# The epsilon of the denominators on VectorE, and a fixed order table in place of a list scheduler, in a fused attention and token-mixing kernel

## The chip, the cores and the metric

The kernel runs on one core of a Trainium2 chip. The metric is the device time of one execution in microseconds (us). The profiled span is about 1.8 us shorter than the device time. Runs come in two states, by the clock that TensorE was granted and by the time: a run over 1.5% above the fastest of the same kernel is called slow, and only fast runs are compared.

Engine names in the profile: PE is TensorE's matmuls, PEld its weight loads, DVE is VectorE, ACT is ScalarE, POOL is GpSimd, SP is SyncE; a q after the name is the engine's issue of DMA transfers. L322 is a line of the source of that kernel, so the same instruction has another number in another kernel.

## The reference, cut to what matters

```python
# q, k, v: (8, 8, 576, 64) float32
def phi(x, c, s):                       # c, s: cos and sin of pi/2 * position / 576
    r = np.maximum(x, 0.0)
    return np.concatenate([r * c, r * s], axis=-1)
kv  = np.einsum('bhsf,bhsd->bhfd', k_p, v)
z   = np.sum(k_p, axis=2)
num = np.einsum('bhsf,bhfd->bhsd', q_p, kv)
den = np.einsum('bhsf,bhf->bhs', q_p, z)[..., None] + 1e-06      # <- the eps of the change
x   = (num / den)  # heads put side by side: (8, 576, 512)
W_tok = 1/8 * (x @ w_q) @ (x @ w_k).T   # written as an einsum
out = relu(W_tok @ x) @ w_out           # (8, 576, 512) float32
```

## The kernel before

Heads are taken in 16 pairs, H = 0 to 15, two of the eight heads of a batch at a time; two pairs at a time feed one of the eight token mixers b, and two mixers feed nine output blocks of 128 rows. The text uses the kernel's own short names:

- **load** of q, v, k (576 KB each, issued by SP); **rq, rv, rk**: relu or cast to bfloat16, on POOL or ACT; **mv**: value times cos and sin, DVE;
- **qT**: transposes of q on PE, **qe**: their eviction with cos and sin, DVE; **kv**: key-value product, **kve** its eviction; **num**: numerators and denominators on PE, **norm**: the division, DVE; **xT, xe**: transposes of x and their evictions;
- **wqk, we, wk, kx, mx, mxe**: the token mixer; **wo.p.n**: output block n of the p-th two mixers, **oe** its eviction to an output buffer, **st** its store; **warm**: dummy matmuls that only keep PE busy.

The eps came from four small matmuls at the end of each num:

```python
    # set up once
    ones_t = consts.tile([P, P], BF16);  nc.gpsimd.memset(ones_t, 1.0)
    eps_t = consts.tile([P, SC], BF16);  nc.gpsimd.memset(eps_t, 0.0)
    # ... two entries a half: EPS_HI and 1.0e-6 - EPS_HI
    def num_mm(H, m):
        # ... 40 matmuls of 64x65 over r, u, w, t, all with stop=False
        for r in range(2):
            for t in range(2):
                nc.tensor.matmul(nb[2 * t + r][:, :, D], ones_t[half_rows(t), :],
                                 eps_t[half_rows(t), :], start=False, stop=True)
    def norm(H, m):
        # ...
        nc.vector.reciprocal(rec, nv[:, :, :, D:D + 1])
        nc.vector.tensor_tensor(xv[:, h], nv[:, :, :, 0:D],
                                rec.to_broadcast([P, 4, SC, D]), op=ALU.mult)
```

The order of the work came from a list scheduler with tuned weights. Every engine, and the queue of loads and stores of SP, executes its part of that order strictly one after another:

```python
    def emit(n, eng, m):           # eng, m: engine and PSUM bank that the scheduler chose
        # ...
        elif kind == "oe":
            wout_evac(b, j, m, engs[eng])
            if b == B // 2 - 1 and j > 4:       # the last four blocks: a store right away,
                lo = (j - 5) % 2                # one half by SP, one by ACT
                store(b, (j + 1) // 2, (nc.sync, A), lo, lo + 1)
        elif kind == "st":
            if b < B // 2 - 1 or j < 3:
                store(b, j, (nc.sync, nc.sync))
        elif kind == "warm":
            warm_up(b, m)
    for n, eng, m in plan_order(NB):
        emit(n, eng, m)
```

## Time and profile before

| quantity | kernel before |
|---|---|
| median of its three first runs | 125.94 us (125.21 to 127.69) |
| the profiled run | 127.62 us, a **slow** one; span 125.8 us, mean clock 0.983 |
| start of kv.4, kv.5, num.15 | 34.80, 42.49, 105.28 us |
| last matmul ends; end of the span | 119.92; 125.84 us |

The start of a PE block in the span, as in the third row, is the ruler: the blocks are the same in both kernels, and where one of them comes later or earlier tells in which stretch the time went.

The profile that the prediction worked from is of a slow run. It has a spell of half clock from 32.8 to 36.2 us, and it is the only profile of this kernel, so whether its fast runs have one is not known. Its times fall roughly into two groups, in all calls: 125.2 to 126.8 and 127.1 to 128.1 us, with one of 130.2.

### The profile page before, as it was taken

What the parts mean: (1) busy time and instruction counts of PE and PEld (TensorE: products, weight loads), DVE (VectorE), ACT (ScalarE), POOL (GpSimd) and SP (SyncE); (2) the same over time, 40 slices, a digit from 0 to 9 for tenths busy, and PEclk for the clock granted to TensorE, in tenths of its full rate; (3) what the DMA queues carried; (4) which work ended last, traced back from release to release, by engine and by line L of the source; (5) the groups of instructions that cost most, each with busy time, mean ns of one, the idle gap of its engine ahead of it and who ended that gap; (6) DMA issues with size and microseconds to landing.
All of it is one profiled execution on the core that took longest, in us unless ns stands there. A gap on an engine that the chain in (4) does not pass through costs nothing.

```text
span 125.8 us, 4659 instructions
## 1 busy us (share of the span) xinstructions
PE 108.5 (86%) x1995; PEld 66.0 (52%) x1995; DVE 82.2 (65%) x90; ACT 83.7 (66%) x141; POOL 70.5 (56%) x113
## 2 busy tenths in 40 slices
PE   5958688688599989999999999999999988998910
PEld 1334454573166756657666666566656664543400
DVE  1064996988928988976878596869597973424000
ACT  5968365565258488786869686967696768756530
POOL 7730557429979998949898898578491000000000
PEclk9999999999779999999999999999999999999998
DMA  3999999999999999999999999999963601567784
GB/s 89 353 395 410 409 363 408 402 410 404 411 408 404 289 300 356 398 411 403 410 397 409 403 404 397 391 401 368 331 223 70 186 2 42 147 150 188 175 247 144
DMA packets 20788, 39.35 MB, mean 313 GB/s; under 512 B 2592, under 2 KB 4128, under 8 KB 20768
## 3 DMA queue, kind: packets, MB, share of 16 engines
q1 hardware_dynamic: 20176, 38.21, 85.2%
q10 hardware_dynamic: 592, 0.85, 2.1%
q8 instruction: 15, 0.25, 0.8%
q14 instruction: 5, 0.04, 0.1%
HBM read 29.62 MB, written 9.44 MB: 310 GB/s over the span
## 4 chain that ended last, share of the span: by engine, by line
PE 60%; DMA 12%; DVE 9%; ACT 9%; issue 2%; ACTq 1%; SPq 1%; POOL 1%; DVEq 0%; POOLq 0%
PE ps L559 25%; PE ps L429 11%; DMA raw<-in_q_dram 7%; PE ps L447 7%; PE ps L489 6%; DMA raw<-in_v_dram 4%; ACT kv_sb L367 4%; PE ps L519 4%; DVE x_sb L462 4%; DVE vp L393 3%; ACT o_sb L367 2%; PE ps L474 2%; PE ps L415 2%; PE ps L535 1%; DVE qpt_buf L421 1%
## 5 line engine op out<-in xcount | busy, mean ns | idle before, releaser
L559 PE MATMUL ps<-wo_sb,mix_sb 128*128 128x512 bf16 x144 | 36.4, 386 | 2.8 <-DVE mix_sb L549 1.4
L380 POOL TENSOR_SCALAR rq_buf<-raw 128x640 bf16<-128x640 f32 (+1 forms) x30 | 20.7, 706 | 14.4 <-DMA raw<-in_q_dram 14.2
L367 ACT COPY o_sb<-ps 128x512 f32<-128x512 f32 x36 | 21.0, 591 | 10.9 <-PE ps L559 9.2
L421 DVE TENSOR_TENSOR qpt_buf<-ps,cst 128x2304 bf16<-128x2304 bf16 x16 | 21.6, 1353 | 10.0 <-PE ps L415 9.5
L393 DVE TENSOR_TENSOR vp<-v_buf,cossin 128x2376 bf16<-128x2376 bf16 (+2 forms) x17 | 23.9, 1409 | 6.0 <-ACT v_buf L403 6.0
L380 POOL TENSOR_SCALAR rk<-raw 128x640 bf16<-128x640 f32 (+1 forms) x26 | 24.6, 964 | 3.2 <-DMA raw<-in_k_dram 1.9
L405 POOL TENSOR_SCALAR v_buf<-raw 128x640 bf16<-128x640 f32 (+1 forms) x28 | 21.4, 782 | 5.6 <-DMA raw<-in_v_dram 2.4
L462 DVE TENSOR_TENSOR x_sb<-ps,rec 128x1280 bf16<-128x1280 f32 x16 | 23.9, 1491 | 0.6
L429 PE MATMUL ps<-vp,rk 64*128 64x260 bf16 x288 | 19.9, 280 | 2.3 <-DVE vp L393 2.3
L559 PEld LDWEIGHTS <-mix_sb 128*128 128x128 bf16 x144 | 12.9, 98 | 17.2 <-issue 3.3
L547 ACT ACTIVATE mix_sb<-ps 128x576 bf16<-128x576 f32 x28 | 18.1, 660 | 2.6 <-PE ps L535 2.6
L367 ACT CAST kv_sb<-ps 128x520 bf16<-128x520 f32 x16 | 9.5, 592 | 13.9 <-PE ps L429 13.6
L429 PEld LDWEIGHTS <-rk 64*128 64x128 bf16 x288 | 13.5, 96 | 9.9 <-issue 2.5
L447 PEld LDWEIGHTS <-qpt_buf 64*128 64x128 bf16 x640 | 11.1, 94 | 4.5 <-issue 4.0
L367 ACT COPY xT_buf<-ps 128x640 bf16<-128x640 bf16 (+1 forms) x21 | 13.1, 655 | 0.4 <-PE ps L474 0.4
L447 PE MATMUL ps<-kv_sb,qpt_buf 64*128 64x65 bf16 x640 | 13.0, 190 | 0.0
L290 PE MATMUL ps<-warm 128*128 128x512 bf16 x35 | 10.6, 448 | 1.5 <-DVE warm L286 1.5
L415 PE MATMUL ps<-ident,rq_buf 64*128 64x64 bf16 x288 | 7.9, 191 | 2.4 <-POOL rq_buf L380 1.7
L489 PE MATMUL ps<-xT_buf,wqk_sb 128*128 128x288 bf16 x64 | 9.4, 286 | 0.0
L369 DVE COPY xT_buf<-ps 128x512 bf16<-128x512 bf16 (+1 forms) x11 | 4.8, 440 | 6.6 <-PE ps L474 5.1
L535 PE MATMUL ps<-wT_buf,kx 64*128 64x288 bf16 x32 | 8.3, 284 | 0.7 <-ACT mix_sb L547 0.4
L535 PE MATMUL ps<-wq,kx 64*128 64x288 bf16 x32 | 8.3, 284 | 0.4 <-ACT wq L367 0.4
(48 smaller groups left out, 94.8 us busy)
## 6 DMA issues: line engine op xcount, KB each, us to landing
raw<-in_q_dram SPq DMA_DIRECT2D x15, 576.0 KB, 8.2
raw<-in_v_dram SPq DMA_DIRECT2D x15, 576.0 KB, 7.3
raw<-in_k_dram SPq DMA_DIRECT2D x15, 576.0 KB, 8.0
out_dram<-o_sb SPq DMA_DIRECT2D x28, 256.0 KB, 5.4
out_dram<-o_sb SPq DMA_DIRECT2D x12, 128.0 KB, 3.6
wo_f<-in_moe_w_out_dram SPq DMA_DIRECT2D x1, 1024.0 KB, 8.4
out_dram<-o_sb ACTq DMA_DIRECT2D x4, 128.0 KB, 2.9
raw<-in_q_dram SPq DMA_DIRECT2D x1, 320.0 KB, 3.9
```

What stands on the lines that cost most here:

```text
L367: nc.scalar.copy(dst, src)
L380: eng.tensor_scalar(dst, src, FMAX, 0.0, op0=ALU.min, op1=ALU.max)
L393: nc.vector.tensor_mul(vp[H][:, 2 * lo:2 * hi], v_bufs[H % 3][:, lo:hi].rearrange("p c i d -> p (c i) d").unsqueeze(2) .to_broadcast([P, 2 ...
L405: eng.tensor_scalar(dst, src, 1.0, 1.0, op0=ALU.mult, op1=ALU.mult)
L421: nc.vector.tensor_mul(qpt_bufs[H % 2][:, :, :, D:SLOTS * D], bank_h(m, 2)[:, :, 0:HC].unsqueeze(2).to_broadcast([P, 2, 2, HC]), cst.unsqu ...
L429: nc.tensor.matmul(bank(m + r)[:, 0, 0:2 * KW], rks[H][half_rows(r), c, :, :], vp[H][half_rows(r), 2 * c:2 * c + 2, :, 0:D + 1], start=(c ...
L447: nc.tensor.matmul(nb[2 * t + r][:, u, :], qpt_bufs[H % 2][rows, r, w, u * P:(u + 1) * P], kvs[H][rows, r, k0:k0 + D + 1], start=(u == 0 a ...
L462: nc.vector.tensor_tensor(xv[:, h], nv[:, :, :, 0:D], rec.to_broadcast([P, 4, SC, D]), op=ALU.mult)
L489: nc.tensor.matmul(bank(m + nh)[:, 0, 0:hs], wqk_sb[:, dmc, :, :], xT_bufs[b % 2][:, dmc, nh * hs:(nh + 1) * hs], start=(dmc == 0), stop=( ...
L535: nc.tensor.matmul(bank(m + r)[:, 0, 0:hs], kxs[b][half_rows(r), i * P:(i + 1) * P], rhs, start=True, stop=True)
L547: nc.scalar.activation(dst, src, AF.Relu, scale=scale_moe)
L559: nc.tensor.matmul(bank(m)[:, 0, :], mixs[bp][:, dmc, rt * P:(rt + 1) * P], wo_sb[:, dmc, :], start=(dmc == 0), stop=(dmc == NDM - 1))
```

## The change

Its intent is to take the eps off PE, the fullest engine, and to replace the scheduler's order by one found offline, by annealing on a replay of the engines.

```diff
-def plan_order(NB, par=None):
-    ... (the list scheduler, some 170 lines)
+NRAW, NOUT = 7, 12
+ORDER = """
+load.q.1=S rq.1=A qT.0=P6 qe.0=V6 warm.3=P0 kv.0=P4 kve.0=A4 load.v.1=S load.k.1=S load.q.2=S
+... (473 items: what=engine and PSUM bank; S is SP's queue)
+... load.q.11=S mxe.2.1=A0 ... oe.0.8=V7 st.0.4=S rk.9=A xT.7=P2 xe.7.1=A3 rq.9=G
+load.v.11=S ...
+wo.3.6=P4 wo.3.7=P5 oe.3.2=A1 oe.3.3=V0 st.3.1=S oe.3.4=V6 st.3.2=S wo.3.8=P6 oe.3.5=V7
+oe.3.6=V4 st.3.3=S oe.3.7=V5 oe.3.8=A6 st.3.4=S
+"""
@@ num_mm
-                            kvs[H][rows, r, k0:k0 + D + 1], start=(u == 0 and w == 0), stop=False)
-        for r in range(2):
-            for t in range(2):
-                nc.tensor.matmul(nb[2 * t + r][:, :, D], ones_t[half_rows(t), :],
-                                 eps_t[half_rows(t), :], start=False, stop=True)
+                            kvs[H][rows, r, k0:k0 + D + 1], start=(u == 0 and w == 0),
+                            stop=(u == SC - 1 and w == 1))
@@ norm
-        nc.vector.reciprocal(rec, nv[:, :, :, D:D + 1])
+        nc.vector.tensor_scalar(rec, nv[:, :, :, D:D + 1], 1.0e-6, 1.0,
+                                op0=ALU.add, op1=ALU.mult)
+        nc.vector.reciprocal(rec, rec)
@@ (also gone: ones_t, eps_t and their six memsets)
-    for n, eng, m in plan_order(NB):
-        emit(n, eng, m)
+    for item in ORDER.split():
+        ... emit(n, on[where[0]], bank)
```

So two things change at once: the **eps part** (PE to DVE) and the **order**.

## The prediction

> **What bounds the kernel now.** I read the page first (engines and slices), then the stretches of the span, then the chain that ended last, then the order of PE's work in time with the start-to-start times of its blocks.
>
> The slices of the page for the kernel before: busy tenths of PE, the granted clock in tenths, and DMA, in slices of 3.145 us.
>
> ```profile
> PE   5958688688599989999999999999999988998910
> PEclk9999999999779999999999999999999999999998
> DMA  3999999999999999999999999999963601567784
> ```
>
> The same by stretches (us, busy us with instruction counts, clock, DMA share, GB/s), cut where the character changes:
>
> ```profile
> core 0: us, PE busy (x) PEld busy (x) DVE busy (x) ACT busy (x) POOL busy (x), PEclk, DMA share, GB/s
> 0.00:34.80 34.80, 26.06 (x460) 14.77 (x461) 23.57 (x26) 20.92 (x28) 20.38 (x51) 0.97 0.99 369
> 34.80:40.24 5.44, 5.43 (x113) 3.70 (x113) 2.81 (x2) 3.99 (x7) 4.71 (x7) 0.87 1.04 406
> 40.24:100.87 60.63, 59.29 (x1235) 38.36 (x1230) 48.95 (x52) 45.29 (x83) 45.47 (x58) 1.00 0.95 344
> 100.87:125.80 24.93, 17.70 (x195) 9.16 (x195) 6.87 (x11) 13.46 (x24) 0.00 (x0) 0.98 0.53 138
> ```
>
> There are three regimes. Up to some 35 us the inputs arrive at the rate of a saturated DMA and PE has holes, filled with dummy matmuls. From 40 to 101 us PE is 98% busy and nothing else is full (DVE 81%, ACT 75%, POOL 75%). From 101 us PE thins out, and after its last matmul (ends at 119.9) come 5.9 us of eviction and store. The chain that ended last shows the hand-overs:
>
> ```profile
> 18.10 9.25 DMA raw<-in_q_dram
> 27.37 0.04 POOLq L380
> ...
> 30.56 1.72 DVE vp L393
> 32.28 0.68 DVE mix_sb L549
> 32.96 0.04 issue
> 33.00 1.87 PE ps L559 x4
> 34.87 1.79 PE ps L429 x13
> ```
>
> The query of head pair 4 lands at 27.35; the loads after it land every 1.4 us (576 KB each, 415 GB/s: key of pair 4 at 30.15, of 5 at 34.48, of 6 at 38.80). PE then stands from 31.65 to 33.00 for one eviction, so that the output block (1.87 us) and the key-value product (1.79 us) run at half clock, against 0.97 and 1.1 us elsewhere in the chain. The end:
>
> ```profile
> 119.85 0.59 ACT o_sb L367
> 120.46 0.49 ACTq L573
> 120.95 0.04 issue
> 120.99 0.59 ACT o_sb L367
> ```
>
> The last eviction starts at 120.99, 1.07 us after its matmuls ended, because ACT alone evicts the last five blocks and issues a store of 0.5 us after each.
>
> [...] half clock for 3.4 us, 32.84 to 36.25, right after the holes of 28 to 33 us. [...] 40 products in 0.63 us, 16 ns each, two row halves at a time. [...] the value multiplication has 1.39 us alone and 1.80 beside POOL work at 30.48.
>
> **The change part by part.** First the eps.
>
> ```profile
> L462 DVE TENSOR_TENSOR x_sb<-ps,rec 128x1280 bf16<-128x1280 f32 x16 | 23.9, 1491 | 0.6
> L460 DVE RECIPROCAL rec<-ps 128x20 f32<-128x20 f32 x16 | 4.4, 277 | 4.3 <-PE ps L453 4.3
> L453 PE MATMUL ps<-eps_t,ones_t 64*128 64x5 bf16 x64 | 3.2, 164 | 0.0
> ```
>
> The 3.2 us of the 64 small matmuls are overlapped lengths. By starts, four of them hold PE some 0.06 us, so 16 x 0.06 = **1.0 us less PE**. DVE gains 16 tensor_scalar of 128x20; I take the reciprocal's 277 ns plus 30 ns of hand-over, so **4.9 us more DVE** in all, 0.3 us in each chain from num to the transpose of x. Six POOL memsets before 5 us go; POOL waits for data after them, so that is worth nothing.
>
> Then the order. I rebuilt the old order from the planner and laid it beside the new table. Loads come in the same sequence up to the key of pair 7, so the landings of the first 43 us stay. After that the new table puts loads ahead of stores. Dummy matmuls fall from 22 to 14 beyond the first 13, all early. Start-to-start times of PE blocks in the full stretch: qT 0.27, kv 1.02, num 0.76, xT 0.27, wqk 1.08, wk 0.15, kx 0.67, mx 0.24, wo 0.93. Over 16, 16, 16, 16, 8, 8, 8, 32 and 36 blocks that is 93.5 us, while PE's span from the first transpose (6.36) to the last block (119.92) is 113.6. So **20 us are lost, most of them before 37 us**; from kv.5 (42.49, work done 19.5, left 74.0) to 119.92 only 3.4 are.
>
> *Head.* I walk the new table with these durations and the old landings. kv.4 needs its cast value (GpSimd 28.75 to 30.1), then the qT eviction (to 30.45) and the value multiplication (to 31.85): kv.4 at 31.9, before 34.80, since the output block no longer stands ahead of it. Then xT.3 at 33.9, wqk.1 at 35.2, num.4 at 36.2. kv.5 waits for DVE's multiplication and starts near 37.35, against 42.49. PE has by then done 16.7 us of work, not 19.5. Net lead: 5.1 - 2.8 = **2.3 us**. About half is the half-clock spell, which I expect to shrink.
>
> *Middle.* The same blocks, less 0.65 us of eps after kv.5; changes of array mode from kv.4 on fall from 59 to 56 (0.3 us at 0.1). But DVE: from 37.3 to norm.15 it has 12 norms of 2.0, 10 qT evictions of 1.28, 10 multiplications of 1.38 and 8.0 us of other evictions (output, x and mix blocks moved there from ACT): 58.6 us. PE has in the same stretch some 59.7. **DVE goes from 81% to nearly full.** I charge 1 us of new stalls.
>
> *Tail.* After num.15 the old order has 13.8 us to the last matmul with 12.6 us of work, because the serial chain norm, xT, wqk, wk, kx, mx outruns the fill. The new one has two more output blocks there, 15 us of work for a chain that grows 0.3: **0.7 us less idle**. The last evictions alternate DVE and ACT, so the last one starts at once: **1.0 us less**.
>
> Sum: 125.9 - 2.3 - 0.65 - 0.3 - 0.7 - 1.0 + 1.0 = 122.95 from measured terms alone. The table was also fitted to the machine, and I allow 1.3 us for stalls of the old middle and the throttle that I can't place: **121.6 us**.
>
> **Rivals.** (a) *DVE becomes the bound*: the 58.6 against 59.7 us above, with PE waiting for norm and the qT eviction in every pair. Against it: before, DVE had 11 us free in the 60. If every new DVE microsecond beyond the slack came through, some 3 us come back and the time is 124 to 125. (b) *DMA sets it anyway*: stores put off pile up in the tail. 39.35 MB at 400 GB/s are 98 us, and DMA was nearly idle from 95 to 110 us, so there is room for eight stores of 1.3 us each. If an output buffer came free late, up to 1 us would be lost. (c) *The head is bound by arrivals and by DVE, not by order*: then kv.5 comes no earlier than about 39, only the tail and eps gain, and the time is near 124. (d) *The fitted order works out as fitted*: the middle loses nothing, and 119 us come.
>
> **Range and chances.** 121.6, with 119.3 to 124.0 for 8 in 10: (d) is the low end, (a) or (c) the high end. Faster by over 2% means below 123.4: 0.77. Within 2%: 0.21, with (a) and (c) together. Slower by over 2% would need a stall in every pair: 0.02.
>
> **What would show it.** Right: no eps matmuls and two 0.28 us DVE steps ahead of each x_sb; kv.4 near 32 and kv.5 near 37.5; hardly any half clock after 33 us; DVE over 90% between 40 and 95; the last eviction within 0.2 us of its matmuls and 5 us or less after the last of them. Wrong: kv.5 after 39; waits of PE on x_sb or qpt_buf of over 3 us in the middle; a DMA wait of ACT or DVE on an output buffer; a half-clock spell in the middle. The weakest number is the 1 us for DVE, since a schedule with two nearly full engines can slip at any late transfer.

## The result, and the profile after

The kernel after took **131.22 us** (median of four, 130.08 to 132.18), against 125.75 us (125.21 to 127.69) for the one before. The ratio is **1.040**, with a 95% interval of 1.030 to 1.050. Ratios here are the mean time of one kernel's fast runs over that of the other's in the same rounds, so they are not quite the ratio of the medians. The change made the kernel slower, by 4%, and the prediction was wrong in direction and range. A repeat with the same source (e0 below) gave 1.0315. The profiled run of the kernel after was a fast one: 131.31 us, span 129.5.

The slices of the page after, in tenths, of 3.24 us each:

```profile
PE   5967634997688999999998883999998999999600
POOL 7524425446799889879100799469585000000000
PEclk9999995599999999999999999599999999999985
DMA  3999999999999999991889999999939850868894
```

Three things are new. Before the last matmul the granted clock drops to half twice: around 20 to 26 us, where PE has just been down to 3 and 4 tenths, and once more in the middle, around 81 to 84 us. DMA has a hole (the 1 in the nineteenth slice, 58 to 61 us) in the time when it had been full. And POOL has a hole right after it (1, 0, 0).

The same by stretches, with the boundaries of the prediction's table (columns as there):

```profile
0.00:34.80 34.80, 24.44 (x440) 14.86 (x446) 23.02 (x30) 22.82 (x31) 17.00 (x38) 0.90 1.00 353
...
40.24:100.87 60.63, 55.26 (x1096) 36.15 (x1111) 50.95 (x61) 43.61 (x77) 40.57 (x53) 0.97 0.93 325
100.87:129.50 28.63, 20.57 (x266) 11.17 (x267) 15.84 (x25) 11.23 (x21) 0.00 (x0) 0.92 0.66 183
```

In the full stretch PE went from 59.29 to 55.26 busy us of 60.63, and DVE only from 48.95 to 50.95. So PE waits more, but not because DVE became full: both have idle time, which is how a chain of waits looks.

Four rulers place the loss. The change that the prediction implied is worked out here from its terms: 5.1 earlier at kv.5; then 2.8 us of work not yet done, less 1.9 for two output blocks moved behind num.15, less 0.65 and 0.3, plus 1.0; and so on.

| stretch | before | after | change | implied by the prediction |
|---|---|---|---|---|
| start to kv.5 | 42.49 | 40.16 | -2.33 | -5.1 |
| kv.5 to num.15 | 62.79 | 66.07 | +3.28 | +0.95 |
| num.15 to the last matmul's end | 14.64 | 15.58 | +0.94 | +1.2 |
| from there to the end of the span | 5.92 | 7.64 | +1.72 | -1.0 |
| span | 125.84 | 129.45 | +3.61 | -3.95 |

The column of before is from a slow run. It can serve nevertheless: e1 below, the old order in a fast run without half clock before its last matmul, has 41.76, 63.15, 14.82 and 5.87. Three stretches are off: the head by 2.8, the middle by 2.3 and the tail by 2.7 us. The causes differ. The rows also bring to light a slip in the prediction itself: its terms add up to 121.95, not to the 122.95 that it states; the 1.3 us of allowance then gives 120.65. The 121.6 lies between.

**The head.** PE's blocks in time, from 19 us; the bracket is PE's idle time just before, and what ended it:

```profile
19.53 0.71 PE L334 MATMUL ps<-ident,x_sb 64*128 64x64 bf16 x18 [2.16 <-DVE x_sb L322]
...
22.50 0.66 PE L276 MATMUL ps<-ident,rq_buf 64*128 64x64 bf16 x18 [1.71 <-ACT rq_buf L239]
22.97 2.14 PE L290 MATMUL ps<-vp,rk 64*128 64x260 bf16 x18
```

PE stands 2.16 us before xT.1 and 1.71 before qT.3, and the half clock runs from 19.32 to 26.15: it sets in at the end of the first of the two stands. The kv block then takes 2.14 us against 1.19 at full clock. A detail is in the last column of the stretches: from 0 to 34.8 us the loads moved 353 GB/s, and 369 in the same stretch before, although SP issues the same loads in the same order.

**The middle.** First the queue of SP, whose instructions are issued one after another; L149 is a load, L433 a store (start, length of the issue):

```profile
53.22 0.37 SPq L149 DMA_DIRECT2D raw<-in_q_dram  x1
60.50 1.38 SPq L433 DMA_DIRECT2D out_dram<-o_sb  x2
61.98 0.61 SPq L149 DMA_DIRECT2D raw<-in_v_dram  x1
```

After the load of q.11 at 53.22 the next item is the store st.0.4. It waits for the eviction oe.0.8, which DVE makes from 59.78 to 60.47. The load of v.11 stands behind it until 61.98, with room for its data. That is the hole in DMA, and it comes out on POOL about ten microseconds later. POOL's work in time:

```profile
60.81 1.29 POOL L241 TENSOR_SCALAR rq_buf<-raw 128x640 bf16<-128x640 f32 x2
71.98 1.29 POOL L241 TENSOR_SCALAR rq_buf<-raw 128x640 bf16<-128x640 f32 x2 [9.87 <-DMA raw<-in_q_dram]
73.24 1.30 POOL L241 TENSOR_SCALAR rk<-raw 128x640 bf16<-128x640 f32 x2
74.61 3.72 POOL L266 TENSOR_SCALAR v_buf<-raw 128x640 bf16<-128x640 f32 x4
```

The table lets POOL do rq.12 before rk.11 and rv.11, so all three wait for a query that landed at 71.81. DVE and PE behind it:

```profile
75.95 1.90 DVE L254 TENSOR_TENSOR vp<-v_buf,cossin 128x2376 bf16<-128x2376 bf16 x1 [1.96 <-POOL v_buf L266]
...
78.29 1.49 DVE L322 TENSOR_TENSOR x_sb<-ps,rec 128x1280 bf16<-128x1280 f32 x1
```

```profile
76.62 0.74 PE L379 MATMUL ps<-x_sb,wkj 128*64 128x256 bf16 x10
79.83 0.28 PE L395 MATMUL ps<-wT_buf,kx 64*128 64x288 bf16 x1 [2.48 <-DVE x_sb L322]
```

The chain reads: v.11 and all loads behind it late, v.11 landing at 68.38 and q.12 at 71.81; POOL idle until q.12, since rq.12 stands first on it; so the cast rv.11, third on POOL, late (74.61), so DVE's multiplication mv.11 late (DVE idle 1.96 us before it), so norm.10, queued behind it on DVE, late; norm.10 is what gives PSUM back to PE, and PE stands 2.48 us. Then the clock is halved from 80.76 to 84.17. POOL's order has a share in this: v.11 had lain there for 6.2 us when its cast began. A run with only rv.11 put ahead of rq.12 was not made.

**The tail.** The last evictions and stores, all engines in time:

```profile
120.02 2.70 ACTq L433 DMA_DIRECT2D out_dram<-o_sb  x3
120.99 0.69 DVE L230 COPY o_sb<-ps 128x512 f32<-128x512 f32 x1 [0.17 <-PE ps L419]
122.84 0.58 ACT L228 COPY o_sb<-ps 128x512 f32<-128x512 f32 x1 [5.05 <-issue]
123.45 0.47 ACTq L433 DMA_DIRECT2D out_dram<-o_sb  x1
```

ACT has no eviction for 5.05 us and still begins the last one 1.03 us after the last matmul, because it first issues three stores, and these wait for DVE's evictions.

**The eps part** by groups of instructions (busy us, mean ns, idle before them); these answer to the prediction's lines of before (the product x_sb is unchanged, 1491 ns):

```profile
L320 DVE RECIPROCAL rec<-rec 128x20 f32<-128x20 f32 x16 | 4.5, 278 | 0.6
L318 DVE TENSOR_SCALAR rec<-ps 128x20 f32<-128x20 f32 x16 | 2.8, 174 | 4.1 <-PE ps L308 3.4 <-PE ps L395 0.4 <-ACT mix_sb L407 0.2
```

The new step takes 174 ns, some 0.20 us from its start to the reciprocal's, so 16 x 0.2 = 3.2 us of DVE in all, and the reciprocal takes the same 278 ns as before. The matmuls for eps are gone.

### The profile page after: what moved, and what is told of

It is laid out like the page before. It is cut to its first block, busy times and chain, and to the rows that moved or that the text cites.

```text
span 129.5 us, 4486 instructions
## 1 busy us (share of the span) xinstructions
PE 104.7 (81%) x1900; PEld 65.4 (51%) x1923; DVE 94.6 (73%) x119; ACT 80.9 (63%) x133; POOL 62.9 (49%) x97
## 4 chain that ended last, share of the span: by engine, by line
PE 60%; DVE 12%; DMA 10%; ACT 3%; POOL 3%; issue 3%; SPq 2%; ACTq 1%; POOLq 0%; DVEq 0%
PE ps L419 24%; PE ps L290 8%; DVE x_sb L322 7%; PE ps L308 7%; PE ps L349 7%; DMA raw<-in_v_dram 6%; DMA raw<-in_k_dram 4%; PE ps L334 4%; PE ps L395 3%; PE ps L379 3%; PE ps L276 3%; SPq L149 2%; POOL rk L241 2%; DVE rec L320 1%; DVE vp L254 1%
## 5 line engine op out<-in xcount | busy, mean ns | idle before, releaser
L419 PE MATMUL ps<-wo_sb,mix_sb 128*128 128x512 bf16 x125 | 34.1, 386 | 1.9 <-issue 1.3
L241 POOL TENSOR_SCALAR rq_buf<-raw 128x640 bf16<-128x640 f32 (+1 forms) x28 | 22.8, 830 | 23.6 <-DMA raw<-in_q_dram 22.9
L322 DVE TENSOR_TENSOR x_sb<-ps,rec 128x1280 bf16<-128x1280 f32 x16 | 23.9, 1491 | 0.6
L266 POOL TENSOR_SCALAR v_buf<-raw 128x640 bf16<-128x640 f32 (+1 forms) x24 | 19.0, 814 | 4.7 <-DMA raw<-in_v_dram 3.9
L241 POOL TENSOR_SCALAR rk<-raw 128x640 bf16<-128x640 f32 (+1 forms) x22 | 17.7, 824 | 7.1 <-DMA raw<-in_k_dram 6.7
L228 ACT COPY o_sb<-ps 128x512 f32<-128x512 f32 x25 | 14.4, 592 | 8.3 <-issue 5.1
L290 PEld LDWEIGHTS <-rk 64*128 64x128 bf16 x288 | 15.0, 97 | 7.1 <-issue 2.6
L228 ACT COPY xT_buf<-ps 128x512 bf16<-128x512 bf16 (+1 forms) x18 | 11.2, 638 | 3.4 <-PE ps L334 3.1
L334 PE MATMUL ps<-ident,x_sb 64*128 64x64 bf16 x288 | 7.9, 197 | 3.2 <-DVE x_sb L322 2.8
L159 PE MATMUL ps<-warm 128*128 128x512 bf16 x23 | 8.4, 497 | 1.8 <-DVE warm L155 1.5
L276 PEld LDWEIGHTS <-rq_buf 64*128 64x128 bf16 x288 | 6.5, 96 | 6.4 <-ACT rq_buf L239 3.2
## 6 DMA issues: line engine op xcount, KB each, us to landing
out_dram<-o_sb SPq DMA_DIRECT2D x12, 128.0 KB, 3.5
out_dram<-o_sb ACTq DMA_DIRECT2D x4, 128.0 KB, 3.5
```

Of the source, the lines that this page charges most:

```text
L228: nc.scalar.copy(dst, src)
L241: eng.tensor_scalar(dst, src, FMAX, 0.0, op0=ALU.min, op1=ALU.max)
L266: eng.tensor_scalar(dst, src, 1.0, 1.0, op0=ALU.mult, op1=ALU.mult)
L276: nc.tensor.transpose(bank_h(m + r)[:, 0, c * D:(c + 1) * D], rq_bufs[H % 3][half_rows(r), c, :, :], ident[half_rows(r), half_rows(r)])
L290: nc.tensor.matmul(bank(m + r)[:, 0, 0:2 * KW], rks[H][half_rows(r), c, :, :], vp[H][half_rows(r), 2 * c:2 * c + 2, :, 0:D + 1], start=(c ...
L322: nc.vector.tensor_tensor(xv[:, h], nv[:, :, :, 0:D], rec.to_broadcast([P, 4, SC, D]), op=ALU.mult)
```

## The experiments

The theory that I went into them with: three faults of the order table cost the time, a store that blocks loads, a cold head, and the tail. Its first rival: the eps step on DVE costs it, since DVE lies in the chain of every head pair. A third cause, that nobody had put into the change, turned up late; e16 to e19 test it. Runs of one call share a chip and the runs of the kernel before: e1 to e4 are the first call, e0, e6, e7, e8 the second, e9, e11, e12, e13 the third, e14 and e15 the fourth, e16 to e19 the fifth. All results were correct. The ratio is that of the fast runs to before's, with its 95% interval. Because before's own runs scatter, its fast mean moved between calls (126.5 us in the second, 126.8 in the fourth, 125.9 in the fifth), so ratios of different calls can differ by 0.7% for that reason alone. The runs of the mended tables lie 0.3 to 2.5 us apart (e7 and e9), and for those I also compare medians. The medians of the table are of all runs; where some were slow, those of the fast runs alone are: after 131.12, e2 127.56, e9 124.46, e17 124.70, e18 129.22, e19 127.95.

| run | median us | ratio to before | interval |
|---|---|---|---|
| after | 131.22 | 1.040 | 1.030 to 1.050 |
| e0 after again | 130.61 | 1.0315 | 1.025 to 1.038 |
| e1 old order, eps on DVE | 127.45 | 1.0109 | 1.004 to 1.018 |
| e2 new order, eps on PE | 127.63 | 1.0113 | 1.004 to 1.018 |
| e3 store behind loads | 128.60 | 1.0185 | 1.010 to 1.027 |
| e4 warm head | 128.03 | 1.0178 | 1.009 to 1.027 |
| e6 last evictions on ACT | 130.17 | 1.0304 | 1.023 to 1.038 |
| e7 = e3 + e4 + e6 | 125.71 | 0.9935 | 0.988 to 0.999 |
| e8 = e7, eps on PE | 123.65 | 0.9774 | 0.972 to 0.983 |
| e9 = e8, early stores | 124.60 | 0.9834 | 0.969 to 0.998 |
| e11 = e7, one more DVE step | 130.11 | 1.0316 | 1.021 to 1.043 |
| e12 = e8, kv.2 first | 123.86 | 0.9803 | 0.970 to 0.991 |
| e13 = e8, wo.3.3 first | 124.07 | 0.9833 | 0.975 to 0.992 |
| e14 = e8, last stores all by SP | 123.65 | 0.9761 | 0.967 to 0.985 |
| e15 = e7, evictions to ACT | 127.96 | 1.0104 | 1.003 to 1.018 |
| e16 = e7, 32 bytes of padding | 124.75 | 0.9914 | 0.988 to 0.995 |
| e17 = e8, 224 bytes of padding | 124.73 | 0.9908 | 0.987 to 0.995 |
| e18 = after, 32 bytes of padding | 129.49 | 1.0259 | 1.020 to 1.031 |
| e19 = e1, 32 bytes of padding | 128.03 | 1.0123 | 1.005 to 1.020 |

### e1 and e2: each part alone

e1 is the kernel before with the change's num_mm and norm; e2 is the kernel after with those of before, its order untouched.

```diff
# e1 (in before)
-        nc.vector.reciprocal(rec, nv[:, :, :, D:D + 1])
+        nc.vector.tensor_scalar(rec, nv[:, :, :, D:D + 1], 1.0e-6, 1.0, op0=ALU.add, op1=ALU.mult)
+        nc.vector.reciprocal(rec, rec)
# ... and the four eps matmuls gone; e2 is the reverse, in after
```

> The old order with eps added on VectorE and no eps matmuls. If the eps on VectorE is what costs (rival: VectorE becomes the bound), 128 to 130 us. If the order costs (my theory), within 1 us of the kernel before (125.75): VectorE was 81% busy in the full stretch, and 16 added operations of 0.17 us (0.20 with the hand-over, 3.3 us in all) fit, with 1 us of PE saved.

> The new table with the eps matmuls of before and the plain reciprocal. If the order costs (my theory): 130 to 131.5 us, at most 1 us less than the changed kernel's 131.2, and the DMA pause near 54 to 60 us is still there. If the eps costs: about 126.

Measured: 1.0109 and 1.0113, so e2 missed both of its expectations (130 to 131.5 and about 126 us), and e1 lies 0.8 us above the median of before in its call. Each part alone costs about 1.1%; together they cost 3.2 to 4.0%, more than the sum of 2.2, though with the intervals of the table the excess over e0's 3.2 is within the noise. e2 still has the blocked queue (SP waits 8.5 us there) and the half clock of the head, from 18.95 to 25.8, but PE's stand in the middle is 1.79 us instead of 2.48, and the clock does not fall after it. So the eps part does not make the faults of the order, it **deepens** them. e1, in the old order, shows no half clock before its last matmul, and its tail is 5.87 us, as before.

### e0: the kernel after once more, as a control

> The changed kernel itself, so that it shares a chip and the runs of before with the next three: 130 to 132 us, ratio 1.03 to 1.05. If its deficit were partly that of one chip, it would come below 1.03.

No edit. Measured 130.61 us, 1.0315: the slowdown is repeated, a little smaller, as expected. Its profile has the head's half clock again (21.3 to 28.1), and a blocked queue (from 53.23 to 61.23 nothing is issued), but PE's stand in the middle is 2.12 us and is not followed by a half clock. So the second cold spell is on the edge and comes in some runs; the first comes in every profile of the table with its own dummies (after, e0, e2, e3, e6, e18).

What goes with it can be read from the clock records of the 20 profiles. Within a run all changes of the clock lie whole multiples of 3.41 us apart (after: 5.67, 19.32, 26.15, 80.76, 84.17). Cut into such stretches of 3.41 us, up to about 105 us, PE was busy 0.94 to 1.76 us in ten stretches at full clock that were followed by half clock, 1.90 us in an eleventh (e3), and 1.77 us or more in every one that was followed by full clock. So it is not the length of a stand alone: that of 2.48 us in the kernel after lies whole in one stretch (77.35 to 80.76), while those of 2.12 us here and of 2.41 us in e18 are divided by an edge (at 79.3 and 78.1), and no half clock follows. The edges lie differently in each run, the first at 4.1 to 7.4 us, so the same order can come out either way.

### e3: the store moved behind the loads

```diff
-... oe.0.8=V7 st.0.4=S rk.9=A ... load.v.11=S ... load.k.11=S ... load.q.12=S ... load.k.12=S ...
+... oe.0.8=V7 rk.9=A ... load.v.11=S ... load.k.11=S ... load.q.12=S ... load.k.12=S st.0.4=S ...
```

> The changed kernel with one entry moved: the store of the last output group of batch pair 0 stands behind the loads of pair 12 instead of ahead of the value of pair 11. Theory of the blocked queue (the store waits 7.3 us for its eviction at the head of the SyncE queue, loads stop, PE later stands 2.5 us and falls to half clock): loads go on at 1.4 us each, GpSimd has no wait of 9.9 us, the half-clock spell at 81 us is gone, and the time falls by 2.5 to 4 us to 127 to 128.7. If the block is hidden (rival): over 130.5.

Measured: 1.0185 and 128.60 us, within the 127 to 128.7 that the theory expected, so 1.3 to 2.2 points less than the table as it was. SP's queue of e3 at the same place:

```profile
53.21 0.37 SPq L147 DMA_DIRECT2D raw<-in_q_dram  x1
54.46 0.37 SPq L147 DMA_DIRECT2D raw<-in_v_dram  x1
```

and its slices of clock and DMA:

```profile
PEclk9999995599999999999999999999999999999975
DMA  3999999999999999999999997899999851959994
```

The load of v.11 is issued at 54.46 instead of 61.98; DMA's hole near 60 us and the second half clock are gone, POOL's longest wait for a query is 3.0 us instead of 9.9, and PE does not stand at the block that it had stood at (mx.3.3 follows kx.4 at once, at 77.32 instead of 79.83). From kv.5 to num.15 e3 takes 62.40 us, against 66.07 in the kernel after and 64.31 in e0, which has the stand but no half clock behind it. By these three profiles some 1.9 of the 3.7 us are the wait itself and 1.8 the cold spell. This shows the mechanism of the middle: one store, of two transfers of 256 KB, 7.5 us too early in an in-order queue. The wait of one store kept the DMA engines nearly empty (59 GB/s in the nineteenth slice of the kernel after) while a load without any wait of its own stood behind it.

### e4: dummy matmuls where PE stands in the head

```diff
-... num.1=P4 norm.1=V4 ... warm.2=P0 qT.3=P4
+... num.1=P4 warm.8=P2 norm.1=V4 ... warm.7=P0 qT.3=P4
```

> The changed kernel with 8 dummy matmuls between num.1 and xT.1 and 7 instead of 2 before qT.3, where PE stood 2.2 and 1.7 us. Theory of the cold head (half clock from 19.3 to 26.2 us costs 2.5 us): no half clock before 30 us, kv.4 near 32.5 instead of 34.3, time 129 to 130. If the head is bound by arrivals and VectorE (rival): half clock gone, kv.4 still after 33.8 and the time within 0.7 us of 131.2.

Measured: 1.0178 and 128.03 us, 1.4 to 2.2 points less and more than the 129 to 130 us expected. The clock by slices:

```profile
PEclk9999999999999999999999998699999999999985
```

The head is at full clock from 20 us on; kv.2 takes 1.18 us instead of 2.14, and kv.4 starts at 32.99 instead of 34.32, kv.5 at 38.75 instead of 40.16. The half clock in the middle (78.83 to 82.24, after a stand of 2.06 us) stays in this profile, which is of the slowest of the four runs (129.43 us, mean clock 0.969); the other three took 127.9 to 128.1 us at mean clocks of 0.981 to 0.989, so they may not have had it. The store's fault is another one and is still there. So 13 more dummy matmuls, which use time in which PE had nothing to do, are worth over 1% here, and the cut of dummies from 22 to 14 was not the saving that it looks like.

### e6: the last evictions back on ACT

```diff
-oe.3.3=V0 ... oe.3.4=V6 ... oe.3.5=V7 ... oe.3.6=V4 ... oe.3.7=V5
+oe.3.3=A0 ... oe.3.4=A6 ... oe.3.5=A7 ... oe.3.6=A4 ... oe.3.7=A5
```

> The changed kernel with the last seven output evictions back on ScalarE, as in the old order; nothing else. In the changed kernel 7.7 us pass from the last matmul to the end, against 5.9: the last eviction stands on ScalarE behind store issues that wait for VectorE, and the last SyncE stores behind their DMA slots. Theory of the tail: 5.9 to 6.2 us again, so 1.5 to 1.8 us less than the changed kernel beside it. If only the last matmul counts (rival: the stores drain at their own rate), under 0.5 us less.

A miss in part. The tail went from 7.64 to 6.70 us, not to about 6, and in time it is 0.4 us by the medians of the same call (130.17 against 130.61), which is about what separates two samples of four here. So the split of the last evictions explains at most 0.9 of the 1.7 us that the tail lost; and as e18 below, with the split as in the kernel after, has a tail of 7.38 us, and e7, without it, one of 7.38 too, not even that is certain.

### e7 and e8: the three mended together, with each eps

e7 has the edits of e3, e4 and e6; e8 is e7 with the eps matmuls on PE and the old norm.

> Store moved behind the loads of pair 12, dummy matmuls in the head, last evictions on ScalarE; eps still on VectorE, the rest of the table as in the changed kernel. If the three places and the eps explain the loss: head 1.3, block 2.5 and tail 1.7 us off 131.2 give about 125.7 (125 to 126.5), the same as before within 1%. If the new table is slower in its body too: over 127.

> The same with the eps matmuls of before. If the eps on VectorE costs where VectorE is on the path (the run with the old order: 1.3 us): 124 to 125, 1 to 1.5 us less than the run beside it and 1% faster than before. If the eps cost only by deepening the stall and the throttle that are now mended: within 0.5 us of it.

Measured: e0 1.0315, e7 0.9935 (125.71 us, as expected), e8 0.9774 (123.65 us, below the 124 to 125 expected). By medians, the three edits are worth 130.61 - 125.71 = **4.9 us**, and the eps part costs 125.71 - 123.65 = **2.1 us** even in the mended order. e8 is 2.3% faster than before (interval 1.7 to 2.8%), the fastest of all runs with e14. From 40 to 100 us PE is busy 58.33 of 60 us in e7 and 58.58 in e8, at full clock (54.62 in the kernel after, 59.05 before), so the table's body, once mended, is as good as the old order's. By the rulers of the result:

| stretch | before | after | e7 | e8 |
|---|---|---|---|---|
| start to kv.5 | 42.49 | 40.16 | 38.75 | 37.29 |
| kv.5 to num.15 | 62.79 | 66.07 | 62.38 | 61.86 |
| num.15 to the last matmul's end | 14.64 | 15.58 | 15.58 | 15.63 |
| tail | 5.92 | 7.64 | 7.38 | 7.49 |
| span | 125.84 | 129.45 | 124.09 | 122.27 |

The difference of e7 and e8 arises early: 0.58 us at xT.1, 1.36 at kv.2, 1.46 at kv.5, and 1.98 at num.15. At kv.2 only two norms have been made, so two steps of 0.2 us. Nearly a microsecond of the 1.36 is not DVE's. What it is, e16 to e19 show.

### e11: the DVE step twice

e7 with a further step of the same size in each norm, which changes nothing in the values:

```diff
         nc.vector.tensor_scalar(rec, nv[:, :, :, D:D + 1], 1.0e-6, 1.0, op0=ALU.add, op1=ALU.mult)
+        nc.vector.tensor_scalar(rec, rec, 1.0, 1.0, op0=ALU.mult, op1=ALU.mult)
         nc.vector.reciprocal(rec, rec)
```

> The table mended in three places, eps on VectorE (125.7 us), and one more VectorE step of the size of the eps step (128x20, times 1) in each norm: 16 x 0.2 = 3.2 us more VectorE, no change on any other engine. If VectorE time before the norms passes into the whole at the rate that removing it did (1.9 to 2.0 us for 3.3 us, with eps matmuls put back at the same time): 127.3 to 128. If that gain was something else, or luck of the clock's phase: under 126.3.

A miss, and an instructive one: 130.11 us against e7's 125.71 (different calls; by ratios 1.0316 against 0.9935), so **4.4 us for 16 x 0.2 = 3.2 us of DVE**. The loss grows through the body: 0.5 us at kv.5, 2.5 at num.9, 4.0 at num.15. From 40 to 100 us DVE is busy 54.15 us of 60, hardly more than in e7 (53.29), and PE falls from 58.33 to 54.35, at full clock. So DVE time is dear in this table, with a loss larger than the added time. How the extra beyond the 3.2 us comes about was not followed to a single wait.

### e15: seven evictions from DVE to ACT

If DVE's sum of work were the bound of e7's body, moving work to ACT, which is at 76%, should help. The evictions oe.0.5, 0.8, 1.1, 1.2, 2.3, 2.5 and kve.5 go from DVE to ACT at the same places of the table.

```diff
-oe.0.5=V1 ... oe.0.8=V7 ... oe.1.1=V2 oe.1.2=V3 ... kve.5=V0 ... oe.2.3=V0 ... oe.2.5=V3
+oe.0.5=A1 ... oe.0.8=A7 ... oe.1.1=A2 oe.1.2=A3 ... kve.5=A0 ... oe.2.3=A0 ... oe.2.5=A3
```

> The mended table with eps on VectorE (125.7), and seven evictions between 39 and 98 us (six output blocks and one of kv) moved from VectorE to ScalarE, 4 us of VectorE in the body and none in the head. If VectorE is full in the body and the added step of 0.2 us in each norm costs there: 124.3 to 125.2. If the eps costs in the head, where norm and the transposes follow each other, and the body had just enough room: within 0.4 us of 125.7.

A miss: 127.96 us, 2.2 us slower than e7 by the medians. From 40 to 100 us DVE falls from 53.29 to 47.42 busy us, and PE falls too, from 58.33 to 55.27. So it is not the sum of DVE's work that sets this body; where each item stands in an in-order engine matters more. It doesn't settle more, as the edit makes ACT's queue late at the same time.

### e9, e12, e13, e14: what else the table might have

All four are e8 with one edit.

```diff
# e9: three put-off stores right after the last load
-... st.0.3=S ... st.1.4=S ... st.1.3=S ...
+... load.k.15=S st.0.3=S st.1.3=S st.1.4=S ...
# e12: kv.2 ahead of qT.3
-... warm.7=P0 qT.3=P4 qe.3=V4 kv.2=P2 ...
+... kv.2=P2 warm.3=P0 qT.3=P4 qe.3=V4 ...
# e13: an output block as a fill before the last mixer
-... mx.7.0=P4 mx.7.1=P6 ... wo.3.3=P0 ...
+... wo.3.3=P0 mx.7.0=P4 mx.7.1=P6 ...
# e14: both halves of the last four stores by SP
-                store(b, (j + 1) // 2, (nc.sync, A), lo, lo + 1)
+                store(b, (j + 1) // 2, (nc.sync, nc.sync), lo, lo + 1)
```

> The mended table with eps matmuls (123.65), and three stores whose data are long ready put ahead of the store that SyncE waits for near 85 to 88 us, instead of behind it. From its last matmul to the end that kernel takes 7.5 us, against 5.9 in the kernel before. If put-off stores jam the tail: tail under 6.5 us and 122.5 to 123. If the last pair's own stores, bunched by a tail with denser matmuls, set it: tail still over 7.2 us and the time within 0.4 us of 123.65.

> The mended table with eps matmuls (123.65), and kv.2 ahead of qT.3 in PE's order, as the old order had it (4 dummy matmuls fewer, so that the gap is filled alike). If the new order of the two costs the head its 1.2 us: num.2 about 1 us earlier and 122.7 to 123.2. If the head is bound by arrivals and VectorE later on: kv.4 and the time within 0.4 us.

> The mended table with eps matmuls (123.65), and the output block 3.3 ahead of the last mixes on PE, as the old order had it, so that its store leaves about 3 us before the next instead of 1.3. If the bunching of the last stores makes the long tail: from the last matmul to the end under 6.7 us and 122.7 to 123.3, although the matmuls may end 0.2 us later. If not: tail over 7.2 us and no gain.

> The mended table with eps matmuls (123.65; 7.5 us from the last matmul to the end), and both halves of the last four stores issued by SyncE instead of half by ScalarE. If the coupling of the two queues through the DMA semaphores sets the tail: no wait of SyncE of over 1 us after 112 us, tail 6.7 to 7.0 and the time 0.4 to 0.8 us less. If the stores drain at the DMA's own rate (rival): tail 7.3 or more, since SyncE now issues 0.6 us x 8 by itself.

None gained anything: 124.60, 123.86, 124.07 and 123.65 us against e8's 123.65, and tails of 7.48, 7.33, 7.37 and 7.38 us against 7.49.

- e9 refutes that the put-off stores jam the tail: with three of them gone earlier the tail is the same.
- e12 brings kv.2 forward (20.36 instead of 21.37), but num.2 stays at 23.69 (23.57 in e8) and kv.5 at 37.35 (37.29): once the clock is kept up, the head is not bound by the order of these PE blocks.
- e13 leaves the tail where it was too.
- e14 tests a coupling seen in the trace of e8: ACT's store issued at 112.84 landed at 117.02, and SP's last four stores, whose data were ready between 112.8 and 116.4, were issued from 117.08 to 118.92, after it; the first of the four waits for the completion of that store of ACT. In e14 no SP wait after 112 us is over 1 us any more, but SP then issues ten stores one after another, from 113.38 to 119.55, at 0.62 us each. The wait became an issue limit, and the time is the same.

So at most 0.9 us of the tail's loss is explained by the split of the evictions (e6), and the rest stays open: whatever I moved there, it came back at 7.3 to 7.5 us in the mended table.

### e16 to e19: where the input buffers lie

The loads gave the clue. GB/s from 2 to 40 us was 393 and 394 in before, e2, e8, e9, e12 and e13 (384 in e14), and 374 to 377 in all nine profiles with eps on DVE, e11 with its doubled step included. So it is not the step. What else the eps part changed is the memory: without the constants ones_t (256 bytes a partition) and eps_t (10 bytes, in a slot of 32) everything allocated after them moves down by 288 bytes. By the placement in the compiled programs, the first of the seven input buffers starts at byte 81408 of a partition before, 318 x 256, and at 81120 after, 224 bytes past a multiple of 256; all seven shift alike, as each is 4608 = 18 x 256 bytes.

That the place of the buffers sets the rate of the loads was my guess; whether it does is for these runs to show. The rates that it has to explain differ by some 4% (376 GB/s against 393). Only two offsets from a multiple of 256 bytes were run, 0 and 224, so that 256 is the step that counts is not shown.

The edit is one unused constant. It moves everything allocated after the constants, the input buffers, the work buffers and the output buffers, and adds one small memset:

```diff
     wo_sb = consts.tile([P, NDM, DM], BF16)
+    pad = consts.tile([P, 16], BF16)        # 32 bytes: e16, e18, e19; [P, 112], 224 bytes: e17
+    nc.gpsimd.memset(pad, 0.0)
```

> e7 (three mended, eps on VectorE) with one unused constant of 32 bytes a partition after the other constants, so that the seven input buffers start again at a multiple of 256 bytes, as they did before the two eps constants were removed; in the change they start 224 bytes past one. Layout theory: what the eps part costs is mostly slower loads (376 GB/s from 2 to 40 us in every profile with eps on VectorE, 393 in every one with it on TensorE except 384 in one): then 393 GB/s here and a ratio of 0.975 to 0.986 to before, near e8. Rival, the VectorE step itself costs it: 376 GB/s or 393, but a ratio near e7's 0.9935.

> The opposite: e8 (three mended, eps on TensorE) with a constant of 224 bytes a partition, so that the input buffers start 224 bytes past a multiple of 256, as in the change. Layout theory: 376 GB/s from 2 to 40 us, a ratio of 0.988 to 0.995. Rival, the VectorE step: no effect, 393 GB/s and 0.977.

> The kernel after as it is, with the same 32 bytes. Layout theory: near the table with the old eps, so 1.010 to 1.020, 393 GB/s, the blocked queue and the cold head still there. Rival, the VectorE step: 1.03 to 1.04.

> The old order with eps on VectorE and the same 32 bytes. Layout theory: 0.994 to 1.003, with 393 GB/s, so that the eps part by itself costs nothing or saves a little. Rival, the VectorE step: 1.011 as in e1.

The stretch from 2 to 40 us (columns as in the tables by stretches; the last is GB/s) in e7, e16, e8 and e17, in this order:

```profile
2.00:40.00 38.00, 31.08 (x578) 18.78 (x578) 28.09 (x35) 26.47 (x38) 20.18 (x33) 1.00 1.05 377
```

```profile
2.00:40.00 38.00, 32.08 (x612) 19.54 (x612) 29.15 (x36) 26.84 (x39) 19.55 (x35) 1.00 1.04 387
```

```profile
2.00:40.00 38.00, 33.30 (x645) 20.63 (x644) 28.79 (x32) 27.37 (x40) 20.21 (x41) 1.00 1.04 393
```

```profile
2.00:40.00 38.00, 31.02 (x606) 19.44 (x604) 27.92 (x31) 26.41 (x38) 21.26 (x40) 1.00 1.05 376
```

The padding changes the rate in both directions, also in the other two: 394 in e18 and e19. In e16 it came back in part only, to 387. The work buffers moved too, but the operations of DVE and ACT last the same in all four, within 1% (1491 or 1492 ns for the division, 592 to 594 for an output eviction on ACT), so it is not the engines' own accesses. What it is worth, in the mended table (medians in us, and starts of blocks):

| | inputs at a multiple of 256 | 224 past one |
|---|---|---|
| eps on PE | e8: 123.65; kv.2 21.37, kv.5 37.29 | e17: 124.73; kv.2 22.94, kv.5 38.35 |
| eps on DVE | e16: 124.75; kv.2 21.73, kv.5 37.69 | e7: 125.71; kv.2 22.73, kv.5 38.75 |

By medians the two effects add up: **the layout costs 1.0 to 1.1 us, the DVE step 1.0 to 1.1 us**. The pairs that share a call say the same: e7 less e8, both effects together, is 2.06 us, and e16 less e17, the step less the layout, is 0.02 us (0.05 with fast runs alone), which gives 1.0 for each if they simply add. The rows and columns are of two calls on two chips; by ratios to before, whose fast mean differed by 0.6 us between the calls, the layout is 1.3% on PE's side and 0.2% on DVE's, so the sizes are good to about half a microsecond, while the direction stands in all. At kv.2 they come apart: the shift is worth 1.0 to 1.6 us there, the two steps 0.36 in one pair and -0.21 in the other. The way is short: in e7 ACT begins rq.3 at 21.24, as soon as its query is there, in e16 at 20.25, and PE waits for it.

So neither theory wins alone, and three of the four ratios that the layout theory expected were missed; the rates came, but for e16's. e17 came as the layout theory had it (0.988 to 0.995). e16's 0.9914 is above its 0.975 to 0.986 and nearer to the rival's figure, as the DVE step keeps half of the cost. e18 has 1.0259, between the two theories: the layout is 1.4 to 1.9 us of the kernel after by the medians of the fast runs (e0 and after against e18), and it still has the cold head and the blocked queue. e19's 1.0123 is the rival's figure, no better than e1's 1.0109: by ratios a gain of the layout in the old order is not shown. e19 fell into two groups, 126.4 to 126.5 (two runs) and 128.0 to 128.8 (four), as before's runs of that call did, 125.6 to 126.3 (five) and 127.6 to 128.1 (six); group against group the step costs some 0.5 us in the old order. The profile of e19 is of the upper group and has a half clock from about 34 us on, as the slow profile of before has; e1, with its slower loads, took 127.4 to 127.6 every time, without one. That the two groups of the old order are the runs with and without that spell is likely, but no profile of a lower one was taken. The mean clocks of before's runs support it in the main: 0.984 to 0.998 in the 18 of the lower group, 0.971 to 0.984 in 19 of the 21 of the upper. But the other two of the upper, at 0.993 and 0.997, have no room for a spell of 3.4 us, which alone takes 1.4% off the mean, so the spell is not the whole difference.

## Why the prediction was wrong, point by point

1. **"Net lead: 5.1 - 2.8 = 2.3 us" in the head: the walk was right, two of its inputs were not.** It had kv.4 at 31.9 and kv.5 at 37.35; e8 has them at 31.84 and 37.29, so it is met to 0.1 us where nothing disturbs it. The kernel after had 34.32 and 40.16. Of the 2.87 us between 40.16 and 37.29, 1.41 came back with the dummies of e4, 1.06 is the layout and 0.40 the DVE step. The first step that failed is "Dummy matmuls fall from 22 to 14", which I counted and did not charge, though I had shown what an idle PE does to the clock. The second is "so the landings of the first 43 us stay": they would have, had the buffers stayed where they were.

2. **"After that the new table puts loads ahead of stores": false at the place that mattered.** I had compared the sequence of loads, but not asked of each store when its data would exist. st.0.4 stands in front of load.v.11 and waits for an eviction 7.3 us later than the load before it. e3 shows that this store alone is worth 1.3 to 2.2%. Two of the prediction's own signs of being wrong came with these two points: kv.5 after 39 (40.16), and a half-clock spell in the middle. My rival (b), stores, looked at the end of the kernel only.

3. **"I charge 1 us of new stalls" for DVE: about right for the step, but it was not all that the eps part did.** The step measured 0.20 us instead of 0.31, so DVE gained 3.2 us rather than 4.9, and it costs 1.0 to 1.1 us net in the mended table and some 0.5 in the old order, where I had expected it to about break even (0.65 us of PE saved, 1 us lost). In the table as it was, e18 against e2 gives 129.22 - 127.56 = 1.7 us by the fast runs of two calls; why it costs more there was not followed. The term that was left out is the line "Six POOL memsets before 5 us go", said to be "worth nothing". With the memsets went their tiles, the input buffers moved by 288 bytes, and that was worth as much again as the step (376 GB/s in e17 against 393 in e8, and 1.08 us). Rival (a), a full DVE, did not come: 50.95 busy us of 60.63.

4. **"The last evictions alternate DVE and ACT, so the last one starts at once: 1.0 us less": wrong in sign.** The last eviction started 1.03 us after its matmuls, as before, because ACT issues stores between evictions, and those now wait for DVE. The alternation couples two engines through ACT's queue. The tail grew by 1.72 us; e6 gives at most 0.9 of that back, and what causes the rest stays open.

5. **The base.** The profile of before was of a slow run, with a half clock that I expected to shrink, "about half" of the head's lead. Most runs of the lower of before's two groups have mean clocks at which no such spell has room, so part of the expected gain was measured against a disturbance that perhaps half the runs don't have.

6. **What held.** The middle was sized well once mended: from kv.5 to num.15 the terms give 62.79 + 0.95 = 63.74, and e7 has 62.38, so a gain of the size of the 1.3 us allowed for the fitted middle is there; that allowance was not derived, and which stalls went was not followed, so the match may be luck. The 0.3 us for changes of array mode rest on 0.1 us a change, the scheduler's own figure; in the profile of before an output block of four matmuls at full clock held PE for 0.86 to 0.88 us when a block with the same array tile (`128*128`) followed it without a stand, and for 0.95 to 0.97 (once 1.10) when one with another did. From num.15 to the last matmul 15.8 were implied, and 15.58 came. The 121.6 was not reached by any mend: e8, with three small mends and the eps left on PE, takes 123.65, and e16, with the eps on DVE as the change has it and 32 bytes of padding, 124.75, still above the range's 124.0.

Taken together, the chances were the fault as much as the terms. I gave 2% to slower by over 2%, on the ground that it "would need a stall in every pair". It needed a few long stalls only, followed by a colder clock, and an in-order queue can make one out of a single item.

## What to carry to other kernels

When an order of work is replaced, check each in-order queue for an item that waits for something late and stands before something that is ready; a store among prefetched loads is the first suspect, and its cost shows far away, here on POOL 10 us later and on PE 17 us later. Count PE's busy time in stretches of 3.41 us and not its longest stand: here PE was busy 0.94 to 1.90 us in those that half clock followed, and 1.77 us or more in the others. Fill such places with dummy matmuls where there is no other work. And when a change removes or adds any buffer, compare the addresses of the transfer buffers before and after, and measure the parts of the change apart: the rate of the loads in the profile would have given it away at once.

## What the runs here show of the hardware

- The granted clock: half clock came with stands of PE of 1.35 us (before, 31.65 to 33.00) to 2.48 us (after), and did not come with those of 2.12 us (e0) and 2.41 us (e18). The spells lasted 3.4 or 6.8 us. What went with them was how long PE was busy in the stretch of 3.41 us just before: 0.94 to 1.90 us, against 1.77 or more where full clock followed.
- Small DVE operations: for 20 elements a partition, 174 ns for tensor_scalar from PSUM, and 277 for reciprocal from PSUM (278 from SBUF), so the operation matters.
- The place of a load's destination: 374 to 377 GB/s from 2 to 40 us where the rows of 2304 bytes start 224 bytes past a multiple of 256, against 384 to 394 where they start at one, and 1.0 to 1.1 us of some 124. Other offsets were not run.
- An in-order issue queue: one waiting store kept ready loads from being issued for 7.3 us. And in the tail of e8 a store of one issuing engine was held until one of another had landed (data ready at 112.8, issued at 117.08, beside a landing at 117.02).
